# Small buffers for moe1's outputs, later requests for set loads, and a new decoding order, in a fused retention and two-MoE kernel

## The chip, the cores and the metric

The kernel runs on one core of one Trainium2 chip. The metric is the device time of one execution in microseconds (us). The core's engines are TensorE (PE in the rows; PEld is its loading of weights), VectorE (DVE), ScalarE (ACT), GpSimd (POOL, idle here) and SyncE (SP, which only asks for transfers). The program lists the instructions of each engine in an order; one that has to wait for another engine holds up those that stand behind it on its own.

## The reference

Three stages follow each other: retention attention over 8 sequences of 576 positions and 8 heads of 64, a first MoE-like block (moe1), and a second (moe2). All inputs are float64 or float32 arrays, results are float32:

```
ret  = (q k^T / 8) * D          # D[i,j] = gamma^(i-j) for i >= j, else 0
x    = ret v                    # as [4608 tokens, 512]
h1   = (x w1) * (x w2)          # [4608, 1024]
x2   = h1 w3 w_out              # [4608, 512]
h    = x2 w_in2                 # [4608, 2048]
out  = (h * clip(h + 3, 0, 6) / 6) w_out2
```

## The kernel before, in words

Every product of float32 matrices is made of three matmuls (`mm3`, lines 124 to 128): each operand is split into a high part, rounded to the type that TensorE reads at full rate, and a low part, the rest; high times high, high times low and low times high are summed in PSUM. The split costs one ScalarE cast (`..h`) and one VectorE subtraction (`..l`, line 131) for each tile.

The weights lie in HBM as 64-bit floats and are decoded on the chip in **pieces** of 128x512 numbers (`weights`, lines 133 to 170). A piece goes through four steps: f0, ScalarE takes the upper word's absolute value (line 146); f1, three VectorE instructions shift and merge the bits (lines 149, 151, 154); f4, ScalarE casts the high part (line 161); f5, VectorE subtracts (line 131). Seven buffers of 128x512 in `stg` and `stg_hi` serve the pieces in turn.

What stands where on each engine is written by hand: `at(s, f)` files a step under tick s, and each `mm3` first runs `tick()`, which emits the steps of the current tick. The first LEAD ticks are emitted before the first matmul, so they are only an order. In all of it the tick is a place in the program, not a time.

The work in order:

- **Prologue** (up to some 115 us): w3 and w_out, 16 + 8 pieces, are decoded, and TensorE makes W = w3 w_out from them (tiles `w3h`, `w3l`, `woh`, `wol`, sum in `Wps`, 64 `mm3`, four to each w3 piece). Between them stand the first three attention excursions (`scores`, `cross`, `pv`, `state`), the making of the decay tables (`make_rates` on VectorE, lines 341 to 358; `make_up` on ScalarE, line 365), and the first pieces of w1.
- **moe1** (some 115 to 860 us): 12 blocks of 384 tokens. For each of 8 column tiles f, `pa` = x w1 and `pb` = x w2 (12 matmuls each), ScalarE copies `pa` out (`a`), VectorE multiplies (`ab`), the product is split (`abh`, `abl`). Then four output tiles `px` (n = 0, 2, 1, 3) are made with W. All of `pa`, `pb`, `px` rotate through four PSUM banks (`ps_mm`). Attention excursions for the block after next stand at three places of each block. w1 and w2 are decoded during block 0; moe2's weights during blocks 1 to 11, through `stg` and `stg_hi` too, and stored to HBM (`wid`, `wqd`).
- **The end of each block**: `x2_copy` (line 541) takes a `px` tile into `stg`; after n = 2 and after n = 3, `x2_sums` makes four differences on VectorE (line 544), `x2_hi` casts seven parts of 192 columns in one ScalarE instruction (line 548), `x2_lo` subtracts them in one VectorE instruction (line 551), and `x2_store` asks for two transfers to `xod` in HBM from ScalarE's queue, one from `stg_hi` and one from `stg`. So each block stores two groups, and the copies of the second group write the place in `stg` from which the first group's transfer reads.
- **moe2** (860 us to the end): h is made by seven products instead of eight on half tiles; eight weight sets of 1.8 MB (`wset`) are held in SBUF, the operands `xop` come back from `xod`. The seven products of a set are named by their place in the order, 0 to 6; product 3 adds onto the bank that `u_copy` has read. `gate` makes the activation: f0, ScalarE's Relu into a buffer `r`; f1, VectorE's multiply; f2, a store to `gd`. The last stage multiplies with w_out2 (`po`).

The memory that `ph1.close()` (line 636) gives back is reused for the sets 5 to 7 and the last `xop`; sets 3 and 4 take the place of w2. All these loads stand on SyncE.

Of the kernel before, what the change touches and what calls it, by code (L numbers as in the profile page):

```python
# [30 lines left out]
def retention_moe_kernel(  # L31
# [20 lines left out]
    nc = tc.nc  # L52
# [40 lines left out]
    def piece():  # L93
        taken[0] += 1
        return pieces[taken[0] % len(pieces)]
# [18 lines left out]
    def at(s, f):  # L114
        slots.setdefault(max(s, now[0]), []).append(f)
# [16 lines left out]

    def weights(key, s_load, s, raw_pool, u, src, hi_lo):

# [33 lines left out]
        at(s_load, f_load)  # L168
        for d, f in enumerate((f0, f1, f4, f5)[:4 if hi_lo else 2]):
            at(s + d, f)  # L170
# [120 lines left out]
    with tc.manual_schedule():  # L291
# [25 lines left out]

        LEAD = 12
        B0 = LEAD + 8 * KF
# [39 lines left out]

        def make_up(s, e):  # L360
            n = 64 if e == 4 or s == 576 else 128
            for p in range(NPAIR):
                for a, rows in enumerate(HALF):
                    h = 2 * p + a
                    nc.scalar.activation(out=up[rows, p, s:s + n], in_=ut[rows, h // 4, h % 4, 0:n],
                                         func=ACTF.Copy, scale=cw[rows, e, h:h + 1])
        woh = wab_p.tile([128, KF, DM], F32R, tag="A2", name="woh")
# [22 lines left out]
        def w3_at(n):  # L390
            return LEAD - 8 + 4 * n

        w3_load = {}
        for n in range(16):
            w3_load[n] = -1 if n < NWR else w3_at(n - NWR) + 2
        first = []
        for n in range(KF):
            weights(("o", n), max(-1, o_at(n) - 12), o_at(n), None, piece(), lambda n=n: load_o(n),
                    lambda n=n: (woh[:, n, :], wol[:, n, :]))
            weights(("3", n), w3_load[n], w3_at(n), wr_p, piece(), w3[n], lambda n=n: hold3(n))  # L400
            if n == 0:
                at(0, lambda: (load_qk(0), load_kv(0), load_tables()))
                at(1, make_rates)
            if n == 2:
                at(0, lambda: (load_qk(1), load_kv(1)))
        for n in range(KF, 16):
            weights(("3", n), w3_load[n], w3_at(n), wr_p, piece(), w3[n], lambda n=n: hold3(n))
        at(o_at(KF - 1) + 3, open_w1)
        at(LEAD + 8, lambda: (load_qk(2), load_kv(2)))
        for i, (s, e) in enumerate(((0, 0), (128, 1), (256, 2), (384, 3), (512, 4), (576, 0))):  # L410
            at(LEAD + 4 + 8 * i, lambda s=s, e=e: make_up(s, e))

        def w12(src, f, s_load, s, tiles_):
            fs = slice(f * 128, f * 128 + 128)
            weights(("1" if src is w1 else "2", f), s_load, s, wf_p, piece(), src[f],
                    lambda: (tiles_[0][:, :, fs], tiles_[1][:, :, fs]))

# [3 lines left out]
        s = LEAD + 8 * KF - 1  # L421
        seq12 += [(s + 1, 0, w2), (s + 3, 1, w2), (s + 7, 5, w1), (s + 11, 2, w2), (s + 17, 3, w2), (s + 23, 6, w1),
                  (s + 27, 4, w2), (s + 34, 7, w1), (s + 38, 5, w2), (s + 44, 6, w2), (s + 50, 7, w2)]
# [3 lines left out]

        ex = {-1: 3, 0: LEAD + 8, 1: LEAD + 24, 2: LEAD + 40}
        for t in range(TPB, NTI):
# [107 lines left out]
        xs = stg[:, 0:8 * HB].rearrange("p (o n) -> p o n", o=8)  # L537

        def x2_copy(n, px):
            o = 0 if n > 1 else 6  # L540
            nc.scalar.copy(out=stg[:, o * HB:o * HB + BLK], in_=px)  # L541

        def x2_sums():
            for o, a, b in ((2, 7, 6), (3, 1, 2), (4, 1, 7), (5, 0, 3)):
                sub(nc.vector, xs[:, o], xs[:, a], xs[:, b])

        def x2_hi():
            nc.scalar.copy(out=stg_hi[:, 0:7 * HB].bitcast(F32R), in_=stg[:, 0:7 * HB])

        def x2_lo():  # L550
            sub(nc.vector, stg[:, 0:7 * HB].bitcast(F32R), stg[:, 0:7 * HB], stg_hi[:, 0:7 * HB].bitcast(F32R))

# [92 lines left out]
        for i in (2, 3):  # L645
            load_set(i + 1, wab_p, WTAGS[i])
        for n in range(5, NSET):
            load_set(n, ap["xl"], f"s{n}")
        tmp = [ap["xl"].tile([128, BLK], F32, name=f"tmp{i}") for i in range(3)]
# [15 lines left out]
        def gate(src, sb, m, half, keep=True):  # L665
            c = {}

            def f0():
                c["r"] = temp("r")
                nc.scalar.activation(out=c["r"], in_=src(), func=ACTF.Relu, bias=three)  # L670

            def f1():
                c["g"] = src() if keep else g_tile()
                nc.vector.scalar_tensor_tensor(
                    out=c["g"], in0=c["r"], scalar=6.0, in1=src(), op0=ALU.min, op1=ALU.mult)

            def f2():
                nc.scalar.dma_start(
                    out=gd[:, m, sb * 2 * BLK:sb * 2 * BLK + 2 * BLK].rearrange(
                        "p (a h n) -> p a h n", a=2, h=2)[:, :, half],  # L680
                    in_=c["g"].rearrange("p (a n) -> p a n", a=2))

            for d, f in ((0, f0), (3, f1), (6, f2)):
                at(now[0] + d, f)
# [209 lines left out]
```

## Time and profile before

| | us |
|---|---|
| median of 3 runs (lowest, highest) | 1632.47 (1632.28, 1642.59) |
| the profiled execution | 1625.79 |
| its span in the profile | 1624.0 |
| TensorE busy in the span | 1537.3 (95%) |
| VectorE busy | 807.0 (50%) |
| ScalarE busy | 521.4 (32%) |

The 16 DMA engines moved 274.87 MB, 169 GB/s over the span. TensorE is the engine that is nearly always busy; the other engines matter where it waits for them. Its clock has two levels, 1.2 and 2.4 GHz; the profile gives the granted share of the higher one (0.5 or 1.0) for any stretch. Over the whole run 0.977 was granted; the low shares lie in the first 120 us and near 810 and 880 us.

### The profile page before, as it was taken

The page shows a single profiled execution, that of the slowest core. Times are in us where ns is not written, and L with a number is a line of the kernel's source. Part 1 is how long each engine was busy: PE and PEld are TensorE (multiplying, and loading weights), DVE is VectorE, ACT ScalarE, POOL GpSimd, SP SyncE. Part 2 cuts the span into 40 slices and gives each one's busy share as a digit, 9 for nine tenths or more (in the row PEclk, how much of TensorE's full clock was granted, in tenths as well). Part 3 has the DMA queues.
Part 4 walks back from the last instruction along what each step waited for, and adds up shares of the span by engine and source line. Part 5 has one row for each costly group of instructions (what it writes and reads, how often), then busy time and mean ns, then how long its engine had stood idle before and what let it go on. Part 6 is the DMA issues. An engine that isn't in the chain of part 4 may idle for free.

```text
span 1624.0 us, 25069 instructions
## 1 busy us (share of the span) xinstructions
PE 1537.3 (95%) x10144; PEld 1424.9 (88%) x10144; DVE 807.0 (50%) x1412; ACT 521.4 (32%) x913; POOL 0.2 (0%) x4
## 2 busy tenths in 40 slices
PE   4689999999999999999796999999999999999999
PEld 3468998999999998999796999999998888888887
DVE  5888455456456355455343666666664222222222
ACT  3654223233223223222122333333332222222222
POOL 0000000000000000000000000000000000000000
PEclk9789999999999999999998999999999999999999
DMA  7545445546436445434558666457494333333221
GB/s 264 191 127 159 147 143 172 167 134 201 160 124 200 142 133 187 153 123 152 185 201 323 230 217 244 168 183 248 163 371 145 130 130 130 130 129 114 101 102 47
DMA packets 179332, 274.87 MB, mean 169 GB/s; under 512 B 12176, under 2 KB 122896, under 8 KB 178192
## 3 DMA queue, kind: packets, MB, share of 16 engines
q1 hardware_dynamic: 76304, 179.41, 32.2%
q10 hardware_dynamic: 102912, 93.87, 17.2%
q8 instruction: 79, 1.29, 0.3%
q14 instruction: 37, 0.30, 0.1%
HBM read 169.94 MB, written 103.28 MB: 168 GB/s over the span
## 4 chain that ended last, share of the span: by engine, by line
PE 79%; DVE 8%; DMA 7%; ACT 3%; issue 2%; SPq 0%; ACTq 0%; DVEq 0%
PE pb L126 10%; PE pb L128 10%; PE pb L127 10%; PE po L128 8%; PE po L126 8%; PE po L127 8%; DMA xod<-stg 6%; PE pa L126 4%; PE pa L128 4%; PE pa L127 4%; PE px L126 2%; PE px L128 2%; PE px L127 2%; PE sc L205 2%; PE z L236 2%; DVE stg L131 2%
## 5 line engine op out<-in xcount | busy, mean ns | idle before, releaser
L131 DVE TENSOR_TENSOR ghl<-gr,ghl 128x512 fp32r<-128x512 f32 x144 | 99.7, 692 | 287.7 <-ACT ghl L768 287.7
L126 PE MATMUL pb<-xop,wset 128*128 128x384 f32 x672 | 226.9, 338 | 13.6 <-ACT stg L703 12.3
L128 PE MATMUL pb<-xop,wset 128*128 128x384 f32 x672 | 226.7, 337 | 0.0
L127 PE MATMUL pb<-xop,wset 128*128 128x384 f32 x672 | 226.6, 337 | 0.0
L128 PE MATMUL po<-wq,ghl 128*128 128x512 f32 x576 | 224.3, 389 | 0.0
L126 PE MATMUL po<-wq,ghl 128*128 128x512 f32 x576 | 224.2, 389 | 0.0
L127 PE MATMUL po<-wq,ghl 128*128 128x512 f32 x576 | 224.1, 389 | 0.0
L768 ACT CAST ghl<-gr 128x512 fp32r<-128x512 f32 x144 | 89.5, 621 | 275.8 <-PE po L128 269.5
L126 PE MATMUL pa<-xh,w1h 128*128 128x384 f32 x384 | 135.2, 352 | 25.2 <-ACT stg L541 23.2
L126 PEld LDWEIGHTS pb<-xop,wset 128*128 128x128 f32 x672 | 126.8, 189 | 15.2 <-ACT stg L703 13.3
L126 PE MATMUL pb<-xh,w2h 128*128 128x384 f32 x384 | 130.8, 341 | 4.4 <-ACT w2h L161 4.4
L127 PE MATMUL pa<-xl,w1h 128*128 128x384 f32 x384 | 131.4, 342 | 0.0
L128 PE MATMUL pa<-xh,w1l 128*128 128x384 f32 x384 | 131.2, 342 | 0.0
L128 PE MATMUL pb<-xh,w2l 128*128 128x384 f32 x384 | 130.7, 340 | 0.3
L127 PE MATMUL pb<-xl,w2h 128*128 128x384 f32 x384 | 130.5, 340 | 0.0
L126 PE MATMUL px<-abh,Wh 128*128 128x384 f32 x384 | 129.5, 337 | 0.0
L670 ACT ACTIVATE stg<-g,three 128x384 f32<-128x384 f32 x144 | 88.9, 617 | 125.2 <-DVE g L660 125.2
L128 PEld LDWEIGHTS po<-wq,ghl 128*128 128x128 f32 x576 | 108.1, 188 | 23.2 <-DVE ghl L131 0.9
L128 PE MATMUL px<-abh,Wl 128*128 128x384 f32 x384 | 128.4, 334 | 0.0
L127 PE MATMUL px<-abl,Wh 128*128 128x384 f32 x384 | 128.4, 334 | 0.0
L126 PEld LDWEIGHTS po<-wq,ghl 128*128 128x128 f32 x576 | 108.1, 188 | 22.8 <-ACT ghl L768 0.5
L127 PEld LDWEIGHTS po<-wq,ghl 128*128 128x128 f32 x576 | 108.1, 188 | 22.5
(108 smaller groups left out, 2383.6 us busy)
## 6 DMA issues: line engine op xcount, KB each, us to landing
gd<-g ACTq DMA_DIRECT2D x192, 192.0 KB, 2.7
gr<-gd SPq DMA_DIRECT2D x72, 512.0 KB, 7.4
xop<-xod SPq DMA_DIRECT2D x42, 768.0 KB, 6.8
qk<-in_qk_dram SPq DMA_DIRECT2D x144, 128.0 KB, 3.9
kv<-in_kv_dram SPq DMA_DIRECT2D x72, 256.0 KB, 3.5
wr<-in_w_dram SPq DMA_DIRECT2D x32, 512.0 KB, 3.6
xod<-stghi ACTq DMA_DIRECT2D x24, 672.0 KB, 5.0
xod<-stg ACTq DMA_DIRECT2D x24, 672.0 KB, 5.7
```

Of the source, the lines that this page charges most:

```text
L126: nc.tensor.matmul(out=out_ap, lhsT=sh, rhs=mh, start=first, stop=False, **kw)
L127: nc.tensor.matmul(out=out_ap, lhsT=sh, rhs=ml, start=False, stop=False, **kw)
L128: nc.tensor.matmul(out=out_ap, lhsT=sl, rhs=mh, start=False, stop=last, **kw)
L131: eng.tensor_tensor(out=out_ap, in0=x, in1=y, op=ALU.subtract)
L205: nc.tensor.matmul(out=sc[js, b, 2 * g + a, :], lhsT=c["kT"][rows, g, a, js], rhs=c["q"][rows, g, a, :], start=True, stop=True, skip_group ...
L236: nc.tensor.matmul(out=c["z"][cols, b, g, :], lhsT=c["v"][:, g, d], rhs=c["P"][:, b, 2 * g + a, :], start=not c["ni"] and g == 0, stop=Tru ...
L670: nc.scalar.activation(out=c["r"], in_=src(), func=ACTF.Relu, bias=three)
L768: nc.scalar.copy(out=h, in_=x)
```

## The change

Three parts of the program are edited, and PE's instructions stay in the order they had.

1. **The prologue's order.** `weights` takes a list of ticks for its four steps, and all pieces of w3, w_out, w1 and w2 use (0, 1, 3, 4) in place of (0, 1, 2, 3). LEAD is 14 instead of 12. The second w_out and w3 pieces are asked for ahead of the first q, k, v and of the tables; `make_rates` stands 8 ticks later and the first scores too; `make_up` is issued for one pair of heads at a time. The first two w2 pieces stand 3 and 1 ticks earlier.
2. **moe1's outputs.** `x2_copy` writes to two buffers of 128x384: a part of `stg` past the columns that are stored, for n = 0 and 1, and a new tile `x2` for n = 2 and 3. The sums read these; `x2_hi` and `x2_lo` become three instructions each, since they read from three places.
3. **moe2's start.** The requests for the sets 3 to 7 are filed 12 ticks later. In the first set of all, the gate's buffer `r` is one of the six rotating `g` tiles and not a part of `stg`.

```diff
-    def weights(key, s_load, s, raw_pool, u, src, hi_lo):
+    def weights(key, s_load, s, raw_pool, u, src, hi_lo, at_=(0, 1, 2, 3)):
...
-        for d, f in enumerate((f0, f1, f4, f5)[:4 if hi_lo else 2]):
+        for d, f in zip(at_, (f0, f1, f4, f5)[:4 if hi_lo else 2]):
             at(s + d, f)
...
-        LEAD = 12
+        LEAD = 14
...
-        def make_up(s, e):
+        def make_up(s, e, p):
             n = 64 if e == 4 or s == 576 else 128
-            for p in range(NPAIR):
...
+            for a, rows in enumerate(HALF):
...
+        AHEAD = (0, 1, 3, 4)
...
-            if n == 0:
+            if n == 1:
                 at(0, lambda: (load_qk(0), load_kv(0), load_tables()))
-                at(1, make_rates)
+                at(9, make_rates)
...
-            at(LEAD + 4 + 8 * i, lambda s=s, e=e: make_up(s, e))
+            for p in range(NPAIR):
+                at(LEAD + 1 + 8 * i + 2 * p, lambda s=s, e=e, p=p: make_up(s, e, p))
...
-        seq12 += [(s + 1, 0, w2), (s + 3, 1, w2), (s + 7, 5, w1), ...
+        seq12 += [(s - 2, 0, w2), (s + 2, 1, w2), (s + 7, 5, w1), ...
...
-        ex = {-1: 3, 0: LEAD + 8, 1: LEAD + 24, 2: LEAD + 40}
+        ex = {-1: 11, 0: LEAD + 8, 1: LEAD + 24, 2: LEAD + 40}
...
+        raw2 = {}
+
         def x2_copy(n, px):
-            o = 0 if n > 1 else 6
-            nc.scalar.copy(out=stg[:, o * HB:o * HB + BLK], in_=px)
+            raw2[n // 2] = (pools["tmp"].tile([128, BLK], F32, tag="x2", name="x2", bufs=1) if n > 1
+                            else stg[:, 8 * HB:8 * HB + BLK])
+            nc.scalar.copy(out=raw2[n // 2], in_=px)
 
         def x2_sums():
-            for o, a, b in ((2, 7, 6), (3, 1, 2), (4, 1, 7), (5, 0, 3)):
-                sub(nc.vector, xs[:, o], xs[:, a], xs[:, b])
+            b1, b2 = raw2[0], raw2[1]
+            b11, b12, b21, b22 = b1[:, 0:HB], b1[:, HB:BLK], b2[:, 0:HB], b2[:, HB:BLK]
+            for o, a, b in ((2, b12, b11), (3, b22, xs[:, 2]), (4, b22, b12), (5, b21, xs[:, 3])):
+                sub(nc.vector, xs[:, o], a, b)
+
+        def x2_parts():
+            return (((0, 2 * HB), raw2[1]), ((6 * HB, 7 * HB), raw2[0][:, 0:HB]), ((2 * HB, 6 * HB), stg[:, 2 * HB:6 * HB]))
 
         def x2_hi():
-            nc.scalar.copy(out=stg_hi[:, 0:7 * HB].bitcast(F32R), in_=stg[:, 0:7 * HB])
+            for (a, b), t in x2_parts():
+                nc.scalar.copy(out=stg_hi[:, a:b].bitcast(F32R), in_=t)
 
         def x2_lo():
-            sub(nc.vector, stg[:, 0:7 * HB].bitcast(F32R), stg[:, 0:7 * HB], stg_hi[:, 0:7 * HB].bitcast(F32R))
+            for (a, b), t in x2_parts():
+                sub(nc.vector, stg[:, a:b].bitcast(F32R), t, stg_hi[:, a:b].bitcast(F32R))
...
         for i in (2, 3):
-            load_set(i + 1, wab_p, WTAGS[i])
+            at(now[0] + 12, lambda i=i: load_set(i + 1, wab_p, WTAGS[i]))
         for n in range(5, NSET):
-            load_set(n, ap["xl"], f"s{n}")
+            at(now[0] + 12, lambda n=n: load_set(n, ap["xl"], f"s{n}"))
...
-                c["r"] = temp("r")
+                c["r"] = g_tile() if (sb, m % NSET) == (0, 0) else temp("r")
```

What it does to the order of the instructions is seen at three places.

**VectorE in the prologue**, two w_out pieces and two w3 pieces (L149, L151, L154 are the three instructions of f1, L131 with `wol` or `w3l` is f5). Before:

```order
L149 TENSOR_SCALAR stghi<-stghi 128x512
L151 SCALAR_TENSOR_TENSOR stghi<-orawA_122,stghi 128x512
L154 SCALAR_TENSOR_TENSOR stghi<-orawA_122,stghi 128x512
L131 TENSOR_TENSOR wol<-stghi,woh 128x512
L149 TENSOR_SCALAR stghi<-stghi 128x512
L151 SCALAR_TENSOR_TENSOR stghi<-wr,stghi 128x512
L154 SCALAR_TENSOR_TENSOR stghi<-wr,stghi 128x512
L131 TENSOR_TENSOR w3l<-stghi,w3h 128x512
```

After:

```order
L149 TENSOR_SCALAR stghi<-stghi 128x512
L151 SCALAR_TENSOR_TENSOR stghi<-wr,stghi 128x512
L154 SCALAR_TENSOR_TENSOR stghi<-wr,stghi 128x512
L131 TENSOR_TENSOR wol<-stghi,woh 128x512
L149 TENSOR_SCALAR stg<-stg 128x512
L151 SCALAR_TENSOR_TENSOR stg<-orawA_122,stg 128x512
L154 SCALAR_TENSOR_TENSOR stg<-orawA_122,stg 128x512
L131 TENSOR_TENSOR w3l<-stghi,w3h 128x512
```

The subtraction that ends a piece stood right behind that piece's own f1; now the neighbour's f1 stands between them.

**ScalarE at the end of a moe1 block** (L541 or L545 are the copies out of PSUM, L548 or L558 the casts, `xod` the stores, L492 or L493 the first copy of the next block), from the second group's copies on. Before:

```order
L541 COPY stg<-px 128x384 x2
L548 CAST stghi<-stg 128x1344
L492 COPY a<-pa 128x384
L555 DMA xod<-stghi 128x7x192
L555 DMA xod<-stg 128x7x192
```

After:

```order
L545 COPY stg<-px 128x384
L545 COPY x_1552<-px 128x384
L558 CAST stghi<-x_1552 128x384
L558 CAST stghi<-stg 128x192
L558 CAST stghi<-stg 128x768
L493 COPY a<-pa 128x384
L566 DMA xod<-stghi 128x7x192
L566 DMA xod<-stg 128x7x192
```

The copies stand where they stood; one cast has become three, and the next block's first copy still stands behind the last of them.

**SyncE at moe2's start**, with what each request waits for (`xop` is the last operand of the first stretch; DMAHW0 to DMAHW7 are eight counters that the program's transfers take in turn, and such a wait is for the transfer that had the counter last). Before:

```order
L617 DMA xop_7883<-xod_66 128x1536 [waits DMAHW2_49,DVE_49,PE_49]
L612 DMA wset_7885<-wid_67 128x3584 [waits DMAHW3_49]
L612 DMA wset_7887<-wid_67 128x3584 [waits DMAHW6_49]
L612 DMA wset_7889<-wid_67 128x3584 [waits DMAHW7_49]
L612 DMA wset_7891<-wid_67 128x3584 [waits DMAHW4_49]
L612 DMA wset_7893<-wid_67 128x3584 [waits DMAHW1_49]
```

After:

```order
L628 DMA xop_8003<-xod_66 128x1536 [waits DMAHW2_49,DVE_49,PE_49]
L623 DMA wset_8060<-wid_67 128x3584 [waits DMAHW4_49]
L623 DMA wset_8062<-wid_67 128x3584 [waits DMAHW6_49]
L623 DMA wset_8064<-wid_67 128x3584 [waits DMAHW2_49]
L623 DMA wset_8066<-wid_67 128x3584 [waits DMAHW5_49]
L623 DMA wset_8068<-wid_67 128x3584 [waits DMAHW1_49]
```

SyncE asks in the same order as before; only the counters differ. In the program before, the fourth set of these (`wset_7891`) waits for the block's last `stg_hi` store, the others for earlier loads or a `gd` store. In the changed one, `wset_8060` and `wset_8062` wait for transfers that ended long before, `wset_8064` for the `xop` just asked for, `wset_8066` for the last `stg` store, `wset_8068` for a `gd` store.

## Rows read from the trace of the kernel before

**Rows 1.** Waits of TensorE, whole run: waited for, us in total, times, longest

```profile
PE Wps L126 <- ACT w3h L161: 25.5, 9, 10.8
PE pa L126 <- ACT stg L541: 23.2, 9, 9.5
PE pb L126 <- ACT stg L703: 12.3, 2, 10.8
...
PE pb L126 <- ACT w2h L161: 4.4, 3, 2.0
```

**Rows 2.** Waits of VectorE from 14 to 117 us

```profile
DVE w3l L131 <- ACT w3h L161: 9.7, 8, 1.9
DVE wol L131 <- ACT woh L161: 4.1, 6, 0.7
```

**Rows 3.** Timeline of VectorE: start, duration, operation [idle before, releaser]

```profile
37.18 0.69 DVE L151 SCALAR_TENSOR_TENSOR stg<-wr,stg 128x512 int32<-128x512 int32 x1
...
41.11 0.42 DVE L149 TENSOR_SCALAR stg<-stg 128x512 int32<-128x512 int32 x1
...
43.67 0.69 DVE L131 TENSOR_TENSOR wol<-stg,woh 128x512 fp32r<-128x512 f32 x1 [0.69 <-ACT woh L161]
44.28 0.42 DVE L149 TENSOR_SCALAR stg<-stg 128x512 int32<-128x512 int32 x1
```

**Rows 4.** Timeline of VectorE at its start

```profile
10.88 0.17 DVE L343 TENSOR_SCALAR cw<-ut 128x8 f32<-128x8 f32 x1 [10.02 <-DMA ut<-in_tables_dram]
...
14.21 0.42 DVE L149 TENSOR_SCALAR stg<-stg 128x512 int32<-128x512 int32 x1
```

**Rows 5.** Timeline of ScalarE in the prologue

```profile
36.56 3.26 ACT L365 ACTIVATE up<-ut,cw 64x128 f32<-64x128 f32 x8
```

**Rows 6.** Timeline of TensorE: ten matmuls apart, twice

```profile
41.12 0.63 PE L127 MATMUL Wps<-wol,w3h 128*128 128x512 f32 x1
...
45.38 0.48 PE L128 MATMUL Wps<-woh,w3l 128*128 128x512 f32 x1
...
91.02 0.39 PE L127 MATMUL Wps<-wol,w3h 128*128 128x512 f32 x1
...
93.30 0.39 PE L128 MATMUL Wps<-woh,w3l 128*128 128x512 f32 x1
```

**Rows 7.** Timeline of ScalarE, VectorE, TensorE at the start of block 2

```profile
251.91 0.48 ACT L541 COPY stg<-px 128x384 f32<-128x384 f32 x1 [10.72 <-DMA xod<-stg]
...
252.42 1.36 DVE L131 TENSOR_TENSOR stg<-stg 128x192 f32<-128x192 f32 x4 [9.64 <-ACT stg L541]
...
252.44 0.45 PE L126 MATMUL pa<-xh,w1h 128*128 128x384 f32 x1 [3.10 <-ACT stg L541]
```

**Rows 8.** Chain of waits in order of time, three stores: start, duration

```profile
794.21 16.50 DMA xod<-stg
...
856.07 4.08 DMA xod<-stg
...
865.13 16.52 DMA xod<-stg
```

**Rows 9.** Stretch: from:to, length, TensorE busy (matmuls), granted clock, DMA share, GB/s

```profile
253.80:257.20 3.40, 3.40 (x12) 0.50 0.32 102
```

**Rows 10.** Timeline of SyncE and TensorE at the start of block 11

```profile
792.24 18.81 SPq L617 DMA_DIRECT2D xop<-xod  x6
...
811.33 0.69 PE L126 MATMUL pa<-xh,w1h 128*128 128x384 f32 x1 [9.46 <-ACT stg L541]
```

**Rows 11.** Timeline of SyncE, ScalarE, TensorE at moe2's start

```profile
860.34 28.06 SPq L612 DMA_DIRECT2D wset<-wid  x5
...
881.73 0.58 ACT L670 ACTIVATE stg<-pb,three 128x384 f32<-128x384 f32 x1 [15.72 <-DMA xod<-stg]
...
884.43 0.69 PE L126 MATMUL pb<-xop,wset 128*128 128x384 f32 x1 [10.77 <-ACT stg L703]
```

**Rows 12.** Stretch, all engines: busy us (instructions) of PE, PEld, DVE, ACT, POOL; clock, DMA

```profile
868.00:872.00 4.00, 4.00 (x25) 4.00 (x24) 0.55 (x1) 0.00 (x0) 0.00 (x0) 1.00 1.04 437
```

More of the change, by code (lines that the diff above doesn't have):

```diff
@@ L358, in make_rates @@
             nc.vector.tensor_scalar(out=cw, in0=cw, scalar1=8.0, scalar2=None, op0=ALU.mult)
-        def make_up(s, e):
+        def make_up(s, e, p):
             n = 64 if e == 4 or s == 576 else 128
-            for p in range(NPAIR):
[L363 to L366, printed above, removed]
+            for a, rows in enumerate(HALF):
+                h = 2 * p + a
+                nc.scalar.activation(out=up[rows, p, s:s + n], in_=ut[rows, h // 4, h % 4, 0:n],
+                                     func=ACTF.Copy, scale=cw[rows, e, h:h + 1])
         woh = wab_p.tile([128, KF, DM], F32R, tag="A2", name="woh")
@@ L398, in retention_moe_kernel @@
             weights(("o", n), max(-1, o_at(n) - 12), o_at(n), None, piece(), lambda n=n: load_o(n),
-                    lambda n=n: (woh[:, n, :], wol[:, n, :]))
-            weights(("3", n), w3_load[n], w3_at(n), wr_p, piece(), w3[n], lambda n=n: hold3(n))
-            if n == 0:
+                    lambda n=n: (woh[:, n, :], wol[:, n, :]), AHEAD)
+            weights(("3", n), w3_load[n], w3_at(n), wr_p, piece(), w3[n], lambda n=n: hold3(n), AHEAD)
+            if n == 1:
                 at(0, lambda: (load_qk(0), load_kv(0), load_tables()))
-                at(1, make_rates)
+                at(9, make_rates)
             if n == 2:
@@ L406, in retention_moe_kernel @@
         for n in range(KF, 16):
-            weights(("3", n), w3_load[n], w3_at(n), wr_p, piece(), w3[n], lambda n=n: hold3(n))
+            weights(("3", n), w3_load[n], w3_at(n), wr_p, piece(), w3[n], lambda n=n: hold3(n), AHEAD)
         at(o_at(KF - 1) + 3, open_w1)
@@ L415, in w12 @@
             weights(("1" if src is w1 else "2", f), s_load, s, wf_p, piece(), src[f],
-                    lambda: (tiles_[0][:, :, fs], tiles_[1][:, :, fs]))
+                    lambda: (tiles_[0][:, :, fs], tiles_[1][:, :, fs]), AHEAD)
         s12 = [LEAD + 42 + 4 * f for f in range(5)]
@@ L421, in retention_moe_kernel @@
         s = LEAD + 8 * KF - 1
-        seq12 += [(s + 1, 0, w2), (s + 3, 1, w2), (s + 7, 5, w1), (s + 11, 2, w2), (s + 17, 3, w2), (s + 23, 6, w1),
+        seq12 += [(s - 2, 0, w2), (s + 2, 1, w2), (s + 7, 5, w1), (s + 11, 2, w2), (s + 17, 3, w2), (s + 23, 6, w1),
                   (s + 27, 4, w2), (s + 34, 7, w1), (s + 38, 5, w2), (s + 44, 6, w2), (s + 50, 7, w2)]
```

## The prediction, made before the changed kernel was run

> **What bounds the kernel now.** I first read the waits of TensorE [rows 1], because it is busy 95% of the span and another engine's change can only give back what TensorE waits. Three places hold nearly all of it: the prologue, where the first matrix product waits for decoded w3 pieces (25.5 us), the start of each moe1 block, where `pa` waits for a copy out of PSUM (23.2 us), and the start of moe2, where it waits for `u_copy` (12.3 us). Then I asked of each what the engine in between was itself waiting for.
>
> In the prologue that is VectorE: from 14 to 117 us it waits 9.7 + 4.1 us just before the subtractions that end a piece [rows 2]. One piece shows why [rows 3]: f1 begins at 41.11, the subtraction stands next in order and starts at 43.67 after 0.69 us of waiting for ScalarE's cast of the same piece, and the next piece begins at 44.28. So a piece takes 3.17 us, of which 2.48 are work. VectorE moreover starts decoding at 14.21, since `make_rates` stands ahead and waits until 10.88 for the tables [rows 4].
>
> At a block's start the copy of the second group out of PSUM waits for the first group's store to have read `stg` (10.72 us idle before it), and TensorE, its four banks full, goes on 0.5 us after that copy began, having lost 3.10 us [rows 7]. Behind such a wait the granted clock is 0.50 for 3.4 us [rows 9]; four stretches of this kind stand in blocks 2 to 8. The worst wait is 9.46 us, at block 11, beside loads that occupy SyncE from 792 to 811 us [rows 10]. At moe2's start ScalarE's first Relu waits 15.72 us for the last store, and TensorE 10.77 us for ScalarE [rows 11]. A store takes 4.08 us where nothing else is loaded and 16.5 beside loads of operands or sets [rows 8].
>
> **The prologue, -16 us.** Before the subtraction of one piece now stands f1 of its neighbour, 1.87 us (43.67 - 0.69 - 41.11), which covers the cast's 0.69. If no wait is left, that returns 13.8 us. The cover needs ScalarE to keep pace: per piece it makes a cast and an absolute value (about 0.65 us each, judged by VectorE's same-sized 0.69) and, now spread out, two of the eight `up` instructions, 3.26 / 4 = 0.82 us [rows 5]. That is 2.1 us against VectorE's 2.48. Eight in one lump made the longer waits of up to 1.9 us in [rows 2], so spreading them is part of the gain. Ahead of `make_rates` VectorE now does three f1 and one subtraction, 3 x 1.87 + 0.61 = 6.2 us, in time that it waited away. The tables come later by two pieces of 0.5 MB, 2.4 us at the 437 GB/s of [rows 12], perhaps 4; net 3 us. Together 16.8; a few w3 pieces still follow each other with nothing between, so I take 16. Bounds: 8, if half of the wait returns as f1 waiting for ScalarE or TensorE being late, and 20, if the start gains all 6.2.
>
> TensorE can follow: ten matmuls take 4.26 us at the low rate and 2.28 at the high [rows 6], so a w3 piece's twelve take 5.1 or 2.7 us, against 5.0 for a w_out and a w3 piece on VectorE.
>
> **Block 0, -1.5 us.** Waits for w2 pieces cost TensorE 4.4 us [rows 1]. In block 0 most subtractions still stand right behind their own f1, because few neighbours are left; the first two pieces come earlier. I take a third. Bounds 0 and 6 (all of the wait and 1.7 us of half clock).
>
> **Blocks 1 to 10, -16 us.** The copies no longer wait for the store; the sums do. They overwrite the stored part of `stg`, so VectorE now waits for the same landing, ScalarE's last cast waits for the sums, and the next block's `pa` copy stands behind that cast. After the landing come the sums, 1.36 us [rows 7], the cast of 768 columns, some 0.95 (half as much again as for 512), and the copy, 0.48: TensorE may go on 2.6 us later than before (0.5 became about 3.1). But it has filled four banks instead of two by then: 24 matmuls more, 24 x 4.00 / 25 = 3.8 us [rows 12], rather 4 since edges are counted. A wait of 3.10 becomes 3.1 + 2.6 - 4 = 1.7; the smaller ones become nothing or tenths. Waits now: 23.2 - 9.46 = 13.7 us, and four half-rate stretches at 3.4 / 2 = 1.7 each, 6.8; in all 20.5. Left: about 3 us of wait and one stretch. The gain is 16; bounds 10 (the waits of all blocks left by half) and 19.5. Two more casts and two more subtractions a group, some 0.1 to 0.2 us each, lie beside matmuls; if that cover went, 22 groups x 0.4 would cost 9 us, which is within the lower bound.
>
> **Block 11, -2 us.** Its loads and store are as before, so only the same exchange applies: 4 us more of filled banks against 2.6 us more of chain. Bounds 0 and 9.
>
> **moe2's start, -7 us.** The later filing hardly delays anything. SyncE does not follow TensorE's ticks; its order is unchanged, and the first two of the five loads wait for nothing that is late. The third waits for the `xop` just asked for, some 4 us; only the fourth waits for the last store, where it waited for a store before, too. So that store still runs beside 3.6 to 5.5 MB of loads, and I leave its 16.52 us. What does help is `r` in a `g` tile: ScalarE passes set 0 and first needs `stg` in set 1. TensorE stops at product 3 of set 2 instead of set 1, 42 matmuls later: 42 x 4.00 / 25 = 6.7 us, with edges 7.3. I take 7. Sets 3 to 7 are not needed before 22 us, so their being later by 4 is covered. Bounds: 3, since `g` tiles of set 0 are free only after `gd` stores that stand behind the slow store in ScalarE's queue, and 14, the 12.3 of [rows 1] and 1.7 of half rate.
>
> Engines move DMA work of two queues by turns, packet by packet (the Trainium skill, "DMA: Bandwidth & Descriptors", section Queues, rings and completion order). If that meant equal shares, a store beside loads would need about twice its lone 4.08 us, 8.2, and moe2's start would gain all 14; [rows 8] show four times, so that the rule does not mean equal bytes here.
>
> **The sum.** 16 + 1.5 + 16 + 2 + 7 = 42.5 us. The profiled execution, 1625.8, would become 1583.3. The median of the runs is 1632.5, 6.7 above it, so I give 1590 for the median.
>
> **Rivals.**
>
> 1. *TensorE becomes the bound in the prologue.* It works in bursts there, and at the low rate a piece takes 5.1 us, more than VectorE's 5.0 for a pair. All 192 matmuls at 0.426 us are 82 us, and three excursions come on top: from a start near 18 us it would end little earlier than now. For it: low-rate stretches after each wait in [rows 6]. Against: the same rows show the high rate once it is kept busy. The prologue gives 4, the time is 1602. "TensorE: Matmul & The Clock Gate" in the Trainium skill, section HAM oscillation, says just this of bursts that end in waits. Chance 0.10.
> 2. *The block waits only change engines.* VectorE, standing in the sums, is late with `ab` of the next block, and the banks of `pb` stay full. If half of the 20.5 us and nothing at block 11 comes back, the time is 1598. Against: `ab` needs only 0.6 us and TensorE is two tiles ahead. Chance 0.06.
> 3. *The stores get through.* If the third set's delay lets moe2's store land some 6 us earlier, its start gives 13, and 1584 results; with block 11 too, 1577. Chance 0.12.
> 4. *Slower: the two engines hinder each other.* They now work at the same time on neighbouring pieces of `stg`. The prologue and block 0 have 40 pieces of 4 VectorE instructions, 160. From 42.5 / 160 = 0.27 us more on each, 0.69 becoming 0.96, the kernel is slower than before; at 0.4 us, 1654. Against: the instruction at 37.18 took its 0.69 us while ScalarE was at work from 36.56 to 39.82 [rows 3, 5]. Chance 0.02.
>
> The forecast keeps 0.70.
>
> **Range and chances.** All lower bounds together give a gain of 21, 1611; all upper ones 68.5, 1564. They will not fall together: 1572 to 1609 holds rivals 1 to 3 and leaves out 2 in 10. A measurement of this kernel tells about 1%, 16 us, from no change. Faster by more: 0.93; within: 0.05; slower by more: 0.02.
>
> **What would show it.** In the changed trace: the waits of `wol` and `w3l` on ScalarE all but gone and the first `pa` 15 to 18 us earlier than 115.4; no wait of the copies on `xod`, but of VectorE's sums; `pa` waits of at most 2 us in blocks 1 to 10, and one of 7 to 9 at block 11; a last store of about 16 us still, with one TensorE wait of some 4 us behind set 1. I am wrong if the prologue ends less than 8 us earlier, or if block starts still lose over 10 us in all.

## The result, and the profile after

The changed kernel takes **1583.94 us** (median of 4 runs, 1583.26 to 1589.62), the kernel before 1633.83 beside it: ratio 0.9692, 95% interval 0.965 to 0.9733. The forecast was 1590. The profiled execution, 1589.62 us, is the slowest of the four; that of before, 1625.79, was faster than every run timed beside it. From profile to profile only 36.2 of the 49.9 us appear, so stages are compared over several profiles here.

Each profile was cut at the start of every block's first `pa`, the end of the last `px` and the end of the last product of a set. The table gives the stages of one profile in us and, in the last column, the median time of all runs of that kernel. What stands behind the sets takes 396.2 to 396.3 us of the span in every profile. The kernel before, timed again beside the later runs, had medians of 1630.4 to 1633.6, so the last column alone does not tell kernels apart that differ by 3 us; and the two profiles of the changed kernel differ by up to 0.7 us in the stages up to block 11 and by 4.6 in the sets.

| kernel | first `pa` | block 0 | blocks 1-10 | block 11 | sets | time |
|---|---|---|---|---|---|---|
| before | 115.4 | 69.1 | 613.0 | 62.4 | 367.8 | 1633.8 |
| changed | 101.7 | 68.3 | 590.9 | 61.1 | 369.6 | 1583.9 |
| changed, second profile | 101.3 | 68.3 | 591.2 | 60.4 | 365.0 | 1584.3 (one run) |
| decoding order alone | 101.5 | 68.3 | 616.2 | 62.4 | 368.2 | 1620.4 |
| small buffers alone | 115.3 | 69.1 | 591.4 | 60.9 | 369.1 | 1602.9 |
| sets later and `r` in `g` alone | 115.7 | 69.1 | 619.4 | 61.0 | 366.0 | 1631.2 |
| straight order in the prologue | 108.7 | 69.9 | 590.9 | 61.1 | 365.8 | 1590.6 |
| excursion behind the third `pa` | 101.4 | 68.4 | 594.1 | 60.7 | 366.0 | 1591.9 |
| set 3 gated | 102.3 | 68.3 | 591.3 | 60.2 | 367.5 | 1586.7 |
| set 0 gated | 103.3 | 68.3 | 590.9 | 63.5 | 366.1 | 1587.2 |
| both gates | 101.8 | 68.3 | 590.5 | 64.1 | 367.6 | 1590.0 |
| sets 3 to 7 paced | 101.4 | 68.2 | 592.1 | 61.1 | 367.5 | 1585.2 |
| sets and block 11 paced | 101.6 | 68.3 | 590.5 | 50.1 | 367.5 | 1575.4 |
| and `xop` later | 101.4 | 68.3 | 590.8 | 50.1 | 361.5 | **1570.1** |

The waits of TensorE over the whole run of the changed kernel (us in total, times, longest), against [rows 1]:

```profile
PE Wps L128 <- DVE w3l L131: 13.7, 8, 4.4
...
PE pb L126 <- DVE tmp L671: 7.8, 2, 5.4
PE pa L126 <- ACT a L493: 7.5, 1, 7.5
...
PE pb L126 <- ACT stg L714: 3.3, 2, 3.0
PE Wps L126 <- ACT w3h L161: 2.9, 4, 1.0
PE pb L126 <- ACT w2h L161: 2.9, 2, 2.0
```

The 23.2 us of `pa` have become one wait of 7.5, at block 11; no row of `pa` from blocks 1 to 10 is left. At moe2's start 7.8 + 3.3 stand where 12.3 stood. Up to the first `pa` TensorE waits 31.3 us in all, where it waited 39.4, and is busy 67.9 us instead of 74.0, at a mean granted clock of 0.90 instead of 0.87. It still waits there for what VectorE and ScalarE make, so the gain is read on VectorE. VectorE's waits from 14 to 101.7 us, against [rows 2]:

```profile
DVE w3l L131 <- ACT w3h L161: 1.7, 3, 0.8
DVE stg L149 <- ACT stg L146: 1.3, 2, 0.7
...
DVE stghi L149 <- ACT stghi L146: 0.6, 1, 0.6
```

Its timeline, against [rows 3, 4] (start, duration, operation, idle before):

```profile
13.53 0.17 DVE L343 TENSOR_SCALAR cw<-ut 128x8 f32<-128x8 f32 x1 [2.36 <-DMA ut<-in_tables_dram]
...
28.76 0.42 DVE L149 TENSOR_SCALAR stg<-stg 128x512 int32<-128x512 int32 x1
29.22 0.69 DVE L151 SCALAR_TENSOR_TENSOR stg<-wr,stg 128x512 int32<-128x512 int32 x1
29.94 0.69 DVE L154 SCALAR_TENSOR_TENSOR stg<-wr,stg 128x512 int32<-128x512 int32 x1
30.55 0.69 DVE L131 TENSOR_TENSOR wol<-stg,woh 128x512 fp32r<-128x512 f32 x1
31.16 0.42 DVE L149 TENSOR_SCALAR stg<-stg 128x512 int32<-128x512 int32 x1
```

A piece now takes 2.40 us from one L149 to the next where it took 3.17, with nothing idle in it, and the instructions are as long as they were (0.69). The tables cost a wait of 2.36 us instead of 10.02.

The start of block 2, against [rows 7], on VectorE, ScalarE and TensorE:

```profile
236.15 0.36 DVE L131 TENSOR_TENSOR stg<-stg 128x192 f32<-128x192 f32 x1 [9.57 <-DMA xod<-stg]
...
238.29 0.47 ACT L493 COPY a<-pa 128x384 f32<-128x384 f32 x1
...
237.41 1.10 PE L205 MATMUL sc<-qk 64*64 64x128 f32 x32
238.45 1.09 PE L236 MATMUL z<-P,kv 128*64 128x128 f32 x16
239.37 0.64 PE L250 MATMUL z<-kv 128*64 128x64 f32 x16
239.93 0.45 PE L126 MATMUL pa<-xh,w1h 128*128 128x384 f32 x1
```

The sums wait for the store's landing, as forecast, and the copy of `pa` starts at 238.29, 2.1 us after they began. TensorE, whose four banks are full at 237.4, has an excursion next in its order and is busy with it until 239.9.

moe2's start, on SyncE, ScalarE, VectorE and TensorE, against [rows 11]:

```profile
822.40 23.64 SPq L623 DMA_DIRECT2D wset<-wid  x5
...
830.83 8.65 ACTq L689 DMA_DIRECT2D gd<-g  x1
839.58 0.61 ACT L681 ACTIVATE g<-g,three 128x384 f32<-128x384 f32 x1 [8.29 <-issue]
...
840.23 0.56 DVE L685 SCALAR_TENSOR_TENSOR g<-g 128x384 f32<-128x384 f32 x1 [6.76 <-ACT g L681]
...
841.31 0.69 PE L126 MATMUL pb<-xop,wset 128*128 128x384 f32 x1 [5.38 <-DVE tmp L671]
```

ScalarE no longer waits for the store at its first Relu, but it stands 8.65 us at the issue of the second `gd` store. VectorE waits for ScalarE, and TensorE for VectorE. TensorE goes on 19.3 us behind the last `px` (841.3 less 822.0), where it went on after 24.5.

### The profile page after: what moved, and what is told of

Its sections match the earlier page's. It is cut to its first block, busy times and chain, and to the rows that moved or that the text cites. A ratio compares the mean times of both kernels' runs of the same rounds, so it can differ in the third digit from the quotient of the medians.

```text
span 1587.8 us, 25148 instructions
## 1 busy us (share of the span) xinstructions
PE 1526.2 (96%) x10144; PEld 1416.9 (89%) x10144; DVE 808.4 (51%) x1460; ACT 527.7 (33%) x961; POOL 0.2 (0%) x4
## 5 line engine op out<-in xcount | busy, mean ns | idle before, releaser
L131 DVE TENSOR_TENSOR ghl<-gr,ghl 128x512 fp32r<-128x512 f32 x144 | 99.7, 692 | 287.6 <-ACT ghl L779 287.6
L128 PE MATMUL pb<-xop,wset 128*128 128x384 f32 x672 | 228.1, 339 | 0.0
L128 PE MATMUL po<-wq,ghl 128*128 128x512 f32 x576 | 224.3, 389 | 0.0
L126 PEld LDWEIGHTS pb<-xop,wset 128*128 128x128 f32 x672 | 127.9, 190 | 13.8 <-DVE tmp L671 8.4
L128 PE MATMUL pb<-xh,w2l 128*128 128x384 f32 x384 | 129.5, 337 | 1.1 <-DVE w2l L131 0.9
L128 PE MATMUL pa<-xh,w1l 128*128 128x384 f32 x384 | 129.9, 338 | 0.0
L128 PEld LDWEIGHTS po<-wq,ghl 128*128 128x128 f32 x576 | 108.1, 188 | 23.2 <-DVE ghl L131 0.9
L126 PEld LDWEIGHTS po<-wq,ghl 128*128 128x128 f32 x576 | 108.1, 188 | 23.1 <-ACT ghl L779 0.5
L128 PE MATMUL px<-abh,Wl 128*128 128x384 f32 x384 | 128.4, 334 | 0.0
L127 PEld LDWEIGHTS pb<-xop,wset 128*128 128x128 f32 x672 | 128.0, 191 | 0.0
```

Of the source, the lines that this page charges most:

```text
L126: nc.tensor.matmul(out=out_ap, lhsT=sh, rhs=mh, start=first, stop=False, **kw)
L127: nc.tensor.matmul(out=out_ap, lhsT=sh, rhs=ml, start=False, stop=False, **kw)
L128: nc.tensor.matmul(out=out_ap, lhsT=sl, rhs=mh, start=False, stop=last, **kw)
L131: eng.tensor_tensor(out=out_ap, in0=x, in1=y, op=ALU.subtract)
```

## The experiments

**The parts, one at a time.** Each kernel is the one before with one part of the diff.

```
decoding order alone: AHEAD, LEAD 14, make_up by pairs, make_rates at 9, w2 pieces earlier
small buffers alone:  x2_copy, x2_sums, x2_parts, x2_hi, x2_lo
sets later alone:     at(now[0] + 12, load_set ...); r = g_tile() in set 0
```

> Only the decoding on neighbouring pieces (order of the pieces' steps, spread `up`, later rates, earlier w2 pieces); the stores and set loads as before. Theory (the three parts add, each in its own stage): the first `pa` stands near 101.7 us as in the changed kernel, 13.7 earlier than 115.4, block 0 is about 1 us shorter, and nothing else moves: 14 to 16 us faster than before, ratio near 0.991. Rival (part of the prologue's gain is only possible with the other parts, or is given back by later waits for stores that now fall into busier times): under 9 us, ratio above 0.9945.

> Only the copies of `px` into the small `x2` buffers; prologue and set loads as before. Theory: `pa` waits at the starts of blocks 1 to 10 are gone and blocks 1 to 11 return 22 to 24 us, ratio near 0.986. The forecast's own size was 16 + 2 us, ratio 0.989, with about 3 us of `pa` waits left. Rival (the waits only change engines, and blocks were shortened by the earlier prologue work): at most 12 us, ratio above 0.9925.

> Only moe2's start: sets 3 to 7 filed 12 steps later and `r` of set 0 in a `g` tile; all else as before. Theory (ScalarE, which also issues the stores of `gd`, is held at their issue behind the slow `xod` stores, so the wait moves from the Relu to the issue): 0 to 4 us faster, ratio 0.9975 to 1.000, last `xod` store still 15 us or more. Rival (the forecast: TensorE's stop comes 7 us later and is shorter): 6 to 8 us faster, ratio near 0.9955.

> The changed kernel once more, for a second profile. Theory: stages up to the end of moe1 repeat within 1 us (first `pa` near 101.7, end of `px` near 822), and what differs between executions is moe2's start, where the order of landings decides: with TensorE waits there of 3 to 11 us, the time is 1583 to 1590. Rival: the difference is spread over all stages.

Measured: 1620.35 us (0.9911, 0.9882 to 0.9939), 1602.93 (0.9808, 0.9781 to 0.9836) and 1631.16 (0.9983, 0.9966 to 0.9999), beside 1633.62 for before. The gains of 13.3, 30.7 and 2.5 us add to 46.5; the whole had 49.9, and the intervals allow for the difference. The first theory held: `pa` at 101.5, though 13.3 us is just under the 14 to 16 expected. The third did: 2.5 us (with an interval that nearly reaches no gain), the last `xod` store at 17.4 us and ScalarE 6.80 us at one `gd` issue. The second was exceeded by 7 us, and the reason is in the two profiles whose code is unchanged in blocks 1 to 10. TensorE's waits there, in the profile of before (184.6 to 797.5 us), in the kernel with the new decoding order alone (169.8 to 785.9 us) and in that with the later sets alone (184.8 to 804.1 us):

```profile
PE pa L126 <- ACT stg L541: 13.8, 8, 3.1
```

```profile
PE pa L126 <- ACT stg L542: 20.0, 9, 3.8
```

```profile
PE pa L126 <- ACT stg L541: 20.3, 9, 4.4
```

The same code lost 6 us more in two other executions, and its blocks took 613.0, 616.2 and 619.4 us. The stores account for it: the ten `stg` stores that these starts wait for took 69.9 us together, from issue to landing, in the profile of before, and 76.3 in each of the other two. With the small buffers the blocks took 590.9, 591.2 and 591.4. So the profile of before was a mild execution of its kernel; the change returned the waits that other executions have, and with them most of what varied.

The second profile of the changed kernel repeats its stages to within 1 us up to the end of `px`, and the sets took 365.0 us instead of 369.6: the theory held.

**What covers the rest of the chain in blocks 1 to 10.** The first excursion of each block is moved behind the third `pa`:

```
-  ex[t] = B0 + SPB * (t // TPB - 1) + 16 + ...
+  ex[t] = B0 + SPB * (t // TPB - 1) + (16 if t % TPB else 20) + ...
```

> The changed kernel, but the first excursion of each block (attention of a later tile) stands after 20 instead of 16 steps of the block, behind the third `pa` instead of before it. Theory (in blocks 1 to 10 the remaining chain of landing, sums, cast and copy is longer than four banks of `pa` and `pb`, 8.3 us, and it is the excursion's 2.6 us that cover the rest): by the stores' durations of 9.4, 9.4, 7.6, 8.0, 8.4, 6.4, 6.9, 10.3, 5.7 and 8.6 us, each less 8.0, `pa` waits of about 6 us in all come back, the longest near 2, with perhaps a half-clock stretch: 6 to 9 us slower than the changed kernel, ratio near 0.974. Rival (the four banks alone suffice): no `pa` wait over 0.5 us, time within 2 us of the changed kernel, ratio near 0.9695.

Measured: 1591.9 us (0.9761, 0.9724 to 0.9798), 8 more than the changed kernel. The waits in blocks 1 to 10 (169.8 to 763.8 us), and the row of the longest but one, in block 2, with the excursion now behind it:

```profile
PE pa L126 <- ACT a L493: 2.0, 3, 0.8
```

```profile
238.16 0.44 PE L126 MATMUL pa<-xh,w1h 128*128 128x384 f32 x1 [0.68 <-ACT a L493]
...
240.46 1.10 PE L205 MATMUL sc<-qk 64*64 64x128 f32 x32
```

Waits on `a` are back in three blocks and the ten blocks take 3.2 us more: the theory's direction, with a third of the waits that it expected, in a profile that was the fastest of the four runs (up to 1599.8). The first stores were shorter than in the changed kernel's profile, 8.9 us at most where that had 10.3. So the excursion covers a part of what four banks do not: 3.2 us are seen; where the median's 8 us went in the slower runs was not profiled.

**The order in the prologue.** The pieces of w_out and w3 get their old distances back, all else as changed:

```
-  weights(("o", n), ..., AHEAD); weights(("3", n), ..., AHEAD)
+  weights(("o", n), ...);        weights(("3", n), ...)
```

> The changed kernel, but the w_out and w3 pieces keep the old distances of their four steps (0, 1, 2, 3 instead of 0, 1, 3, 4), so that VectorE's subtraction stands right behind the same piece's decoding again; start, `up` and w1, w2 pieces as changed. Theory (the neighbour's decoding covers the cast): VectorE waits for the casts of `w3h` and `woh` again, 24 pieces by 0.4 to 0.7 us, the first `pa` comes 9 to 13 us later than at 101.7, time about 1594 to 1597, ratio near 0.977. Rival (the gain came from the earlier start and the spread `up`): first `pa` at most 5 us later, ratio below 0.973.

Measured: 1590.58 us (0.9754, 0.9714 to 0.9793), first `pa` at 108.7. VectorE's waits from 14 to 108.6 us:

```profile
DVE w3l L131 <- ACT w3h L161: 5.2, 7, 0.8
DVE wol L131 <- ACT woh L161: 2.7, 4, 0.7
```

It lies between theory and rival: the neighbour is worth 7.0 us of the 13.7, less than the 9 to 13 expected. The order of the steps brings back 7.9 us of waits for the casts, where [rows 2] had 13.8, and the longest is 0.8 where it was 1.9. The spread `up` is the likely reason for the rest, since in the profile of before the waits above 0.8 us stand behind its lumps; no run spreads `up` alone.

**moe2's start: requests behind the store.** Set 3's load waits for a memset of one of its columns that VectorE reaches 12 steps into moe2:

```
+  if late: nc.vector.memset(w[:, 0, 0:1].bitcast(F32), 0.0)   # only for set 3
   nc.sync.dma_start(out=w.bitcast(F32), in_=wid[n])
```

> The changed kernel, but set 3's load waits for a one-column memset that VectorE reaches 12 steps into moe2, so that sets 3 to 7 are really asked for some 4 us behind the last `xod` stores. Theory (ScalarE stands 8 us at the issue of a `gd` store because the slow `xod` stores are ahead of it, and they are slow because they share the DMA engines with the set loads): the two stores land 4 to 6 us after their issue, no issue of ScalarE takes over 2 us, TensorE's waits of 5.4 and 3.0 us and two stretches at half clock go: 8 to 11 us faster than the changed kernel, about 1574, ratio near 0.9635. Rival (the loads, 4 us later, now meet the `gd` stores, or set 3 comes too late): ScalarE is held again, gain at most 3 us, ratio above 0.9675.

Measured: 1586.72 us (0.9721, 0.9696 to 0.9746), no gain. The DMA issues from 822 to 862 us (KB each, median us to landing), first of the changed kernel, then of this one:

```profile
gd<-g ACTq DMA_DIRECT2D x12, 192.0 KB, 8.4
xod<-stghi ACTq DMA_DIRECT2D x1, 672.0 KB, 17.9
xod<-stg ACTq DMA_DIRECT2D x1, 672.0 KB, 18.7
```

```profile
gd<-g ACTq DMA_DIRECT2D x12, 192.0 KB, 11.3
...
xod<-stg ACTq DMA_DIRECT2D x1, 672.0 KB, 4.7
```

and this kernel's waits of VectorE (821 to 862 us) and, apart, of TensorE from 810 us on:

```profile
DVE g L687 <- DMA gd<-g: 7.0, 1, 7.0
DVE g L673 <- DMA gd<-g: 6.2, 1, 6.2
```

```profile
PE pb L126 <- ACT stg L716: 8.2, 3, 4.4
PE pb L126 <- DVE stghi L673: 1.8, 1, 1.8
```

The first steps of the theory happened: the store lands in 4.7 us and ScalarE is held nowhere (none of its twelve `gd` issues up to 862 us takes over 0.8 us). Yet TensorE waits 10.0 us instead of 11.1. The set loads now meet the `gd` stores, which land in 11.3 us, and VectorE waits for their `g` tiles. My theory fell. Its rival held in what it said of the loads and the time, but it is VectorE and not ScalarE that is held: the wait moved from one store to the next.

**Block 11: its loads behind the store.** Set 0, with the six `xop` loads behind it in SyncE's queue, gets the same gate; then both gates together.

```
-  load_set(0, ap["xr"], "s0")
+  load_set(0, ap["xr"], "s0", True)      # gated, filed 4 steps into block 11 as before
```

> The changed kernel, but set 0's load, and behind it the six `xop` loads, wait for a one-column memset that VectorE reaches 4 steps into block 11, after the sums that wait for the store. Theory (the 7.5 us `pa` wait at block 11 is the store's 17 us beside these loads): the store lands in 5 to 9 us, the wait is gone with the half-clock stretch behind it, 8 to 10 us faster than the changed kernel, about 1575, ratio near 0.964; the loads then meet block 11's own store, which nobody waits for within 40 us. Rival (the loads' bytes are only moved into something that waits): moe2 starts later or block 11 loses elsewhere, gain at most 3 us.

> Both gates together. Theory: the two places are 50 us apart and independent, so the gains add: 16 to 20 us faster than the changed kernel, about 1565, ratio near 0.958. Rival (the first gate pushes the loads of sets 1 and 2 and of the `xop` into moe2's start): under 12 us, ratio above 0.962.

Measured: 1587.17 us (0.9727, 0.97 to 0.9754) and 1590.01 (0.9741, 0.9711 to 0.977): no gain, and 6 us lost with both. In the first, waits of TensorE and then of ScalarE from 760 to 800 us, and two rows of SyncE's timeline:

```profile
PE pb L126 <- DVE ab L504: 11.3, 1, 11.3
```

```profile
ACT stg L146 <- DMA wr<-in_w_out_dram: 15.9, 1, 15.9
```

```profile
766.57 4.67 SPq L630 DMA_DIRECT2D xop<-xod  x6
775.78 7.15 SPq L103 DMA_DIRECT2D wr<-in_w_out_dram  x2
```

The `pa` wait is gone. The six `xop` loads, which have no gate of their own, are asked for 11 us later too (766.57 instead of 755.60), so they are still landing when a w_out2 piece (`wr`) is asked for behind them, at 775.8 as against 774.5 in the changed kernel. The piece lands 13.7 us after its request, where it took 8.0. ScalarE stands 15.9 us before the piece's first step, with the cast of `abh` behind it, and TensorE 11.3 (16.1 and 11.4 with both gates). Both theories fell to a wait that I had not named, that for a later load of the queue in which the gate stands; the first one's rival had only said that block 11 might lose elsewhere.

**One load at a time.** First sets 3 to 7 are each gated, 14 steps apart; then also, in block 11, set 0 and the `xop` loads, 8 steps apart:

```
+  at(now[0] + 12 + 14 * (i - 2), lambda i=i: load_set(i + 1, ..., True))     # sets 3, 4; 5 to 7 alike
+  at(now[0] + 8 + 8 * i, lambda i=i: load_xop(0, i, True))                   # second kernel
-  at(E0 + 4, open_late)
+  at(E0 + 12, open_late)                                                     # second kernel
```

> The changed kernel, but each of sets 3 to 7 waits for a one-column memset of its own, 14 steps (one set's products, 6.9 us) apart, from step 12 on: one load of 1.8 MB at a time. Theory (a small store on ScalarE's queue lands only when the loads in flight on SyncE's queue have drained; with two sets in flight that is 13 us, with one it is 4 to 7): the `gd` stores of sets 0 and 1 land in 2 to 8 us, no `g` tile is waited for over 3 us, TensorE's waits behind moe2's start fall from 10.8 us to under 3, no half-clock stretch there: 8 to 11 us faster than the changed kernel, about 1574, ratio near 0.964. Rival (sets 5 to 7 now land too late, or a single load starves the stores as well): waits on `wset` or `g` of 4 us or more, gain under 3 us, ratio above 0.968.

> The same, and in block 11 set 0 and the six `xop` loads are asked for one by one, 8 steps (4.1 us) apart from step 12 on, each behind a memset of its own, so that no piece of w_out2 stands behind all of them in SyncE's queue. Theory: the first store lands in 5 us, the 7.5 us wait at block 11 is gone and no wait of 11 us takes its place as in the kernel with one gate: 15 to 19 us faster than the changed kernel, about 1567, ratio near 0.959. Rival (the block's own store, the decoding and the loads still meet): block 11 stays at 61 us or more, ratio above 0.9635.

Measured: 1585.18 us (0.9714, 0.9669 to 0.9758) and 1575.43 (0.9657, 0.962 to 0.9694). At moe2's start the rival held once more: with `xop` loads of the second pair in between, `gd` stores still took 8.9 us in the median (822 to 862 us), and TensorE waited 9.9 (from 810 us on):

```profile
PE pb L126 <- ACT stg L716: 6.9, 4, 3.4
PE pb L126 <- DVE tmp L673: 2.0, 1, 2.0
PE pb L126 <- DMA wset<-wid: 1.0, 1, 1.0
```

At block 11 the theory held: the block took 50.1 us instead of 61.1, and from its start to its end the trace has no wait of TensorE. The 11.0 us are the wait of 7.5 and half of the 6.8 us at half rate that stood behind it in the changed kernel (from 774.4 us); no such stretch is left. The total stayed above the expected 1567 by what the sets did not give. The store that the block's start waits for, asked for at 756.25 us, landed in 4.4 us (issues from 754 to 757.5 us), against 17.3 in the changed kernel:

```profile
xod<-stg ACTq DMA_DIRECT2D x1, 672.0 KB, 4.4
```

**Fewer bytes in the same stretch.** Four `xop` loads of the second pair are asked for after set 5 instead of set 2:

```
-  if k == 2:
+  if k == (5 if sb == 0 else 2):
```

> The kernel with both paced loads, but the first four `xop` loads of the second pair of blocks are asked for after set 5 instead of after set 2, behind all set loads. Theory (what holds moe2's start is the bytes that must pass in it: a `gd` store waits for whatever SyncE has in flight, and with sets paced one by one it is the `xop` loads that make two in flight): `gd` stores of sets 1 and 2 land in 9 us instead of 11 to 12, TensorE's waits of 3.7 and 3.4 us shrink, the set stage falls from 367.5 to 361 to 364 us, time about 1570, ratio near 0.962. Rival (a set load alone takes as long as a set's products, so the wait only moves to sets 3 to 7 or to the second pair): the stage stays at 366 us or more, time 1573 to 1577, ratio near 0.9655.

Measured: 1570.11 us (0.9629, 0.9587 to 0.967), the sets in 361.5 us. The waits of TensorE from 810 us to the end, first of the kernel with both paced loads, then of this one:

```profile
PE pb L126 <- ACT stg L718: 7.8, 4, 3.7
PE pb L126 <- DMA wset<-wid: 0.6, 1, 0.6
```

```profile
PE pb L126 <- ACT stg L718: 5.9, 5, 2.3
PE pb L126 <- ACT x L545: 0.6, 1, 0.6
```

Stage and time came out as the theory said, 6.0 us less in the sets than with both paced loads. Of these, 2.5 are waits; most of the rest is the clock. The kernel with both paced loads had two stretches at half rate here, of 3.4 and 6.8 us, and this one, with waits of at most 2.3 us, has none: its granted clock is 1.00 from 810.6 to 900 us. The sign that the theory named came in part: the `gd` stores of set 2 landed after 4.2 to 5.7 us instead of 6.6 to 12.1, but those of set 1 took 8.8 to 12.4 instead of 10.6 to 12.0. So taking 3 MB out of the stretch helped, where moving the requests within it had not; whether it is the bytes or the number of loads in flight beside a store, and whether it helps without the pacing, no run tells. This kernel is faster than the changed one: its runs lie between 1568.3 and 1576.3, those of the changed kernel between 1583.3 and 1589.6.

## Why the prediction was right, and where its sizes were off

- **Prologue, 16 forecast, 13.7 measured**, and so under the 15 to 18 that were named as a sign. By its steps: the start gained 3.5 us (`make_rates` ends 2.65 us later with 6.2 us of decoding done ahead), where 3 net was forecast. Of the 13.8 us of waits for casts 1.7 stayed, and 1.9 returned as L149 waiting for ScalarE's absolute value, so 10.2 came back; 10.2 + 3.5 is the measured sum. The working said that the spread `up` was part of the gain but gave it no share. The run with the straight order gives the neighbour 7.0; beside the start's 3.5 that leaves 3.2, which would be the spread `up`.
- **Block 0, 1.5 forecast, 0.8 measured**; TensorE's waits for w2 pieces went from 4.4 to 2.9 + 0.9 (L128).
- **Blocks 1 to 10, 16 forecast (at most 19.5): 22 between the two profiles, and 29 by the runs** (30.7 less the 1.5 of block 11). The mechanism was right, two of its terms were mis-sized. "Waits now ... 13.7 us" was one lucky execution; two others have 20.0 and 20.3. And "left: about 3 us of wait and one stretch" counted only two more banks as cover: nothing is left. The excursion at step 16 of each block lay in the order and adds some 2.5 us (237.41 to 239.93) just where the banks are full; moving it brought waits back. Waits and half of the half-rate stretches (3.4 us each) account for nearly all that the old blocks took beyond the changed ones: 20.6 of 22.1 us in the profile of before (four stretches), 23.4 of 25.3 with the new decoding order alone (two), 27.1 of 28.5 with the later sets alone (four).
- **Block 11, 2 forecast, 1.3 measured.** It has no excursion, and one wait of 7.5 us stayed; 7 to 9 had been said.
- **moe2's start, 7 forecast, some 2 measured, under the lower bound of 3** (2.5 alone in the runs; in the profiles 367.8, 368.2 and 369.1 with the old start, 369.6, 365.0 and 366.0 with the new). The step that failed is "ScalarE passes set 0 and first needs `stg` in set 1". It passed the Relus of set 0 but not the issue of its own `gd` stores, which the working had at nothing. TensorE stopped 13.9 us behind the last `px` (841.3 less its wait of 5.4, less 822.0), where it had stopped after 13.7 (884.4 less 10.8, less 859.9). In its own order that is 12 matmuls later, at product 5 of set 1, where product 3 of set 2, 42 later, had been forecast. The lower bound spoke of the `gd` stores behind the slow store, but as a wait for `g` tiles. Removing the hold did not help either; what holds the start then is the stores beside the loads.
- **The sum.** 42.5 forecast against 1625.8, 49.9 measured between medians. The 6.7 us between profile and median were carried over to the changed kernel as a constant. They were not: by the profiles of the parts they were mostly block waits that this execution happened not to have, and the change removed them. That 1590 came within 6 us of the measured time is in part luck: 13 us too little in blocks 1 to 10 stand against 2.3 too much in the prologue, 0.7 each in blocks 0 and 11, and some 5 at moe2's start.
- **Rivals.** TensorE was not the bound in the prologue: it still waits for `w3l`, `Wl` and `w3h` there. ([rows 6], named for this rival, show the two rates but no wait before them.) The block waits did not change engines: TensorE has none left in blocks 1 to 10. VectorE did not slow down: its same-sized steps took 691 to 694 ns before and after, 0.27 us more being the break-even. The third rival (stores get through) did not happen: the last two landed in 17.9 and 18.7 us.

On turns by packet I read the rule of the Trainium skill ("DMA: Bandwidth & Descriptors", section Queues, rings and completion order) as equal shares and set it aside. The trace shows how the bytes were shared. The queues of SyncE (q1) and ScalarE (q10) from 824 to 841.5 us in the changed kernel (packets, MB, share of time):

```profile
q1 hardware_dynamic: 548, 6.12, 84.9%
q10 hardware_dynamic: 1205, 0.91, 15.4%
```

A load's packet carries 11.2 KB here and a store's 0.75, so the stores got few bytes, 0.91 of 7.03 MB, although they had 2.2 packets for each of the loads'. Equal turns by these packets would give as many of one as of the other, so the row does not show the rule. It does not refute it either, since nothing shows that the page's packets are these and no run changed a packet's size. Why a store beside loads is slow stays open.

## What to carry to other kernels

Before a wait is costed from one profile, ask how it varies: here a wait that depends on when a store lands was 13.8 us in one execution and 20 in two others, and its removal returned more than the first. To find what covers a chain, read the consumer's whole order past the point where it used to stop, not only the buffers. And where every rearrangement of transfers only renames the wait, try to move some of them out of the stretch; a gate on a load also holds all that stands behind it in its queue.

## What the runs showed of the hardware

- An engine can stand in the issue of a DMA. With the two `xod` stores of 672 KB still under way on ScalarE's queue, the issue of its second `gd` store took 8.65 us (9.65 and 9.51 in two other profiles, 6.80 with the sets later alone), and all of ScalarE's work behind it waited; with those stores landed (set 3 gated), no such issue up to 862 us took over 0.8, the median being 0.37. What the queue's limit is, no run measured.
- A store beside loads landed when the loads did. At moe2's start the `xod` stores landed in 3.6 to 4.8 us where no set was being loaded and in 16.2 to 18.9 beside set loads, 1 to 3 us behind the third of the sets asked for (before: 879.7 and 881.6 us against 878.6; changed: 842.2 and 844.0 against 841.1). In the kernel with set 3 gated, the first `gd` stores of 192 KB took 13.0 us beside two sets; their median over the whole run of the changed kernel is 2.9.
